# The first MoE block in full fp32 on whole decoded weights, norm sums in banks of their own, weight loads as steps of their own, and a new order

## The chip, the core and the metric

One NeuronCore of a Trainium2 chip. Its engines work side by side, each through its own queue in order: TensorE (PE; its weight loads are shown apart, as PEld), VectorE (DVE), ScalarE (ACT), GpSimd (POOL), and SyncE (SP), which issues most of the DMAs. The metric is the device time of one execution in microseconds (us).

## What is computed

Attention with a delta rule over 768 steps for 4 x 8 heads of 48 features, and two MoE blocks on the 3072 tokens that come out of it:

```python
k_n = k / (np.linalg.norm(k, axis=-1, keepdims=True) + 1e-06)
for t in range(S):                       # S = 768, state 48 x 48 per head
    y[:, :, t] = einsum('bhd,bhde->bhe', q[:, :, t], state)
    v_old = einsum('bhde,bhd->bhe', state, k_n[:, :, t])
    state = state + beta_t * einsum('bhd,bhe->bhde', k_n[:, :, t], v_t - v_old)
# first MoE block: d_model 384, d_ff 2048
h = x @ w_in
g = where(h >= 1, h, where(h <= -1, 0, (h + 1) ** 2 / 4))
x = g @ w_out
# second: d_ff 1536
xn = x / sqrt(mean(x * x) + 1e-06) * rms_g
out = (silu(xn @ w_gate) * (xn @ w_val)) @ w_out
```

The MoE weights arrive as 64-bit floats and are decoded to fp32 on the chip.

## The kernel before

**Attention.** The 768 steps are cut into 12 chunks of 64. A unit `u` is one chunk of one half of the heads (p = u % 2, chunk c = u // 2). Groups of units (`GRP`: 0-1, 2-3, then four at a time) share their coefficients. `a_ss` forms the squared norms of k, `a_coef` the root, reciprocal and coefficients, `a_gram` the products k k^T (`gk`), `inverse` (POOL, groups from 2 on) or `inv16` and `inv_t` (groups 0 and 1) the inverse of a triangular matrix, `a_mz` and `a_mw` its second half (`mg`). The state goes on from chunk to chunk: `b_gs` (`gs`), `b_tr` (`tr`), `b_x` (`px`, the chunk's output), `b_ds` (the state), and `b_xT` turns the output over (`xps`) into the tokens `xh`, `xl` of the MoE.

**First MoE block** (`m1`). Tokens go in blocks `BLK`: block 0 is chunk 0 (256 tokens), block 1 is chunk 1, then two chunks (512 tokens) at a time. For each of 16 slices f of d_ff: a first half, `mm_in`, 3 contraction steps into `hps`; ACT and DVE form `g`; a second half, `mm_out`, 3 products into `acc`. Every fp32 product is made of three fp32r products (`mm3`): high x high, high x low, low x high. So weights, tokens and `g` are split into a high and a low part. Block 0's products are 256 columns wide.

**Weights.** `w_dec` loads one weight tile (SP), forms it with three copies on ACT and one instruction on DVE (`dy`), then its high part (ACT or DVE) and low part (DVE or POOL). There are 32 tiles for the first block (`w[1, f, i]`, i = 0 for the first half, 1 for the second) and 36 for the second, which go back to DRAM.

**Second block** (`m2`). Products of 512 columns (`gv`, `acc`), paced by PE.

**Order.** A planner (`Flow`) writes the order of all this. Each step names its engine, a cost, what it needs and which buffers it takes and frees; a step's priority is its place in the program plus a number of the table `PLACE`; `CHAIN` names the first steps of a kind that go ahead of all. The order is then fixed: each engine works through its queue and waits where an operand isn't there. Where the planner sees a gap on PE ahead of the MoE, `spin` puts filler products (`warm`) there. `early` makes a tile of the pool `wp` (32 buffers), which later holds the weights.

## Time and profile before

| | before |
|---|---|
| timed runs (3), median and ends | 1093.87 us (1091.93 to 1099.88) |
| the profiled execution | 1093.34 us |
| its span in the trace | 1091.6 us |
| mean granted TensorE clock | 0.987 |
| busy: PE, DVE, ACT, POOL | 1070.5, 614.2, 526.0, 301.4 us |
| HBM read, written | 83.33, 32.77 MB |

Busy time of PE counts filler products, and the ends of its matmuls are modelled: a busy PE isn't PE at its peak. What a stage is bound by is read from the windows and the timelines of that stage, from the start of one instruction to the start of the next. In the trace a full fp32 product makes two records (x32 are 16 products), an fp32r product one.

### The profile page before, as it was taken

The numbers are of one execution on the slowest core, as the hardware profiler recorded it, in microseconds if no ns is written. First come the engines' busy times: TensorE is split into PE (matmuls) and PEld (weight loads), VectorE is DVE, ScalarE is ACT, GpSimd is POOL, SyncE is SP. The second block draws the span as 40 slices with busy tenths as digits, with TensorE's granted clock in tenths as the row PEclk, the third lists the DMA queues.
The fourth block names the chain that finished last, engine by engine and source line by source line (L and its number), as shares of the span: only waits on it lengthen the run. The fifth ranks groups of instructions, "written<-read, shape, count | busy, mean of one in ns | idle before, by whom it ended". The sixth has DMA issues, their size and how long they took to land.

```text
span 1091.6 us, 23723 instructions
## 1 busy us (share of the span) xinstructions
PE 1070.5 (98%) x9804; PEld 894.6 (82%) x9804; DVE 614.2 (56%) x1068; ACT 526.0 (48%) x999; POOL 301.4 (28%) x500
## 2 busy tenths in 40 slices
PE   8888999999999999999999999999999999999998
PEld 6678899878888878888888888888888888888887
DVE  5788998676687666755555533633333333333332
ACT  4787876556567656555666532522222122222221
POOL 5769587286683862011000000000000000000000
PEclk8998899999999999999999999999999999999999
DMA  9794456855648445334224930110010010010000
GB/s 285 261 290 129 76 163 224 215 161 141 159 144 167 143 121 171 95 106 122 102 73 166 343 109 10 39 39 20 1 39 20 1 49 11 20 39 0 29 1 30
DMA packets 140876, 117.64 MB, mean 108 GB/s; under 512 B 97120, under 2 KB 106976, under 8 KB 140768
## 3 DMA queue, kind: packets, MB, share of 16 engines
q1 hardware_dynamic: 120208, 113.50, 34.4%
q10 hardware_dynamic: 20560, 2.62, 1.6%
q8 instruction: 77, 1.26, 0.5%
q14 instruction: 31, 0.25, 0.1%
HBM read 83.33 MB, written 32.77 MB: 106 GB/s over the span
## 4 chain that ended last, share of the span: by engine, by line
PE 87%; DVE 4%; POOL 4%; ACT 2%; issue 2%; DMA 0%; SPq 0%; POOLq 0%; DVEq 0%; ACTq 0%
PE acc L884 10%; PE acc L885 10%; PE acc L886 10%; PE gv L886 9%; PE gv L885 9%; PE gv L884 9%; PE hps L884 6%; PE hps L885 5%; PE hps L886 5%; PE gs L748 3%; PE tr L824 2%; POOL xi L659 2%; POOL tmp L653 2%; PE gk L512 2%; PE px L837 2%
## 5 line engine op out<-in xcount | busy, mean ns | idle before, releaser
L884 PE MATMUL acc<-g,w 128*128 128x512 f32 (+1 forms) x552 | 209.4, 379 | 2.8 <-ACT da L356 2.8
L886 PE MATMUL acc<-g,w 128*128 128x512 f32 (+1 forms) x552 | 205.4, 372 | 0.3 <-DVE w L372 0.2
L885 PE MATMUL acc<-g,w 128*128 128x512 f32 (+1 forms) x552 | 205.5, 372 | 0.0
L884 PE MATMUL gv<-fix,w 128*128 128x512 f32 x432 | 168.2, 389 | 0.0
L886 PE MATMUL gv<-fix,w 128*128 128x512 f32 x432 | 168.2, 389 | 0.0
L885 PE MATMUL gv<-fix,w 128*128 128x512 f32 x432 | 168.2, 389 | 0.0
L901 ACT ACTIVATE g<-fix 128x512 fp32r<-128x512 f32 x72 | 45.4, 631 | 213.3 <-PE acc L886 207.4
L884 PE MATMUL hps<-xh,w 128*128 128x512 f32 (+1 forms) x336 | 127.1, 378 | 1.8 <-DVE s L924 1.8
L902 DVE TENSOR_TENSOR g<-fix,g 128x512 fp32r<-128x512 f32 x72 | 49.9, 693 | 133.1 <-ACT g L901 133.1
L884 PEld LDWEIGHTS acc<-g,w 128*128 128x128 f32 x552 | 104.3, 189 | 22.2 <-ACT da L356 3.0
L885 PE MATMUL hps<-xl,w 128*128 128x512 f32 (+1 forms) x336 | 122.3, 364 | 0.0
L886 PE MATMUL hps<-xh,w 128*128 128x512 f32 (+1 forms) x336 | 122.2, 364 | 0.0
L886 PEld LDWEIGHTS acc<-g,w 128*128 128x128 f32 x552 | 104.3, 189 | 18.8 <-DVE w L372 0.7
L885 PEld LDWEIGHTS acc<-g,w 128*128 128x128 f32 x552 | 104.4, 189 | 16.8
L921 ACT ACTIVATE s<-hps 128x512 f32<-128x512 f32 (+1 forms) x112 | 59.7, 533 | 104.4 <-PE hps L886 86.7
L924 DVE TENSOR_TENSOR s<-s,hps 128x512 f32<-128x512 f32 (+1 forms) x112 | 67.9, 607 | 68.2 <-ACT s L922 67.0
L1132 DVE TENSOR_TENSOR fix<-fix,gv 128x512 f32<-128x512 f32 x72 | 49.5, 688 | 87.4 <-ACT fix L1131 87.4
L653 POOL TENSOR_TENSOR tmp<-nt,xi 128x31 f32<-128x31 f32 (+15 forms) x155 | 92.9, 599 | 20.3 <-DMA nt<-scr_a 8.7
L659 POOL TENSOR_TENSOR xi<-xi,tmp 128x31 f32<-128x31 f32 (+15 forms) x155 | 93.9, 606 | 12.1
L932 DVE TENSOR_TENSOR g<-s,g 128x512 fp32r<-128x512 f32 (+1 forms) x111 | 78.8, 716 | 29.6 <-ACT g L930 28.8
L885 PEld LDWEIGHTS gv<-fix,w 128*128 128x128 f32 x432 | 81.1, 188 | 16.9
L884 PEld LDWEIGHTS gv<-fix,w 128*128 128x128 f32 x432 | 81.1, 188 | 16.8
(186 smaller groups left out, 1673.3 us busy)
## 6 DMA issues: line engine op xcount, KB each, us to landing
wst<-in_w SPq DMA_DIRECT2D x68, 384.0 KB, 5.4
w2d<-wst SPq DMA_DIRECT2D x36, 384.0 KB, 4.6
w<-w2d SPq DMA_DIRECT2D x36, 384.0 KB, 3.7
kvb<-in_kv SPq DMA_DIRECT2D x24, 384.0 KB, 3.7
kt<-in_kqT SPq DMA_DIRECT2D x22, 256.0 KB, 4.7
scr_a<-al SPq DMA_DIRECT2D x20, 256.0 KB, 5.9
xn_d<-x SPq DMA_DIRECT2D x12, 384.0 KB
xn<-xn_d SPq DMA_DIRECT2D x18, 256.0 KB, 3.7
```

What stands on the lines that cost most here:

```text
L653: nc.gpsimd.tensor_tensor(out=tv, in0=nt[:, m:32, j:m].to_broadcast([w, n, m]), in1=x[:, j:m, 0:m].to_broadcast([w, n, m]), op=ALU.mult,)
L659: nc.gpsimd.tensor_tensor(out=x[:, m:32, 0:m], in0=x[:, m:32, 0:m], in1=tv, op=ALU.add)
L748: nc.tensor.matmul(out=ps[half(b), h, 0:n], lhsT=kt[u][half(1 - b), 4 * k + h, :], rhs=qs[p][half(1 - b), b, 4 * k + h, 0:n], start=True, ...
L884: nc.tensor.matmul(out=out, lhsT=wh, rhs=xh, start=first, stop=False, skip_group_check=shared)
L885: nc.tensor.matmul(out=out, lhsT=wh, rhs=xl, start=False, stop=False, skip_group_check=shared)
L886: nc.tensor.matmul(out=out, lhsT=wl, rhs=xh, start=False, stop=last, skip_group_check=shared)
L901: nc.scalar.activation(out=hi, in_=src, func=ACTF.Copy)
L902: nc.vector.tensor_tensor(out=lo, in0=src, in1=hi.bitcast(F32), op=ALU.subtract)
L921: nc.scalar.activation(out=s, in_=ps, func=IDENTITY_SAT240, scale=240.0)
L924: nc.vector.tensor_tensor(out=s, in0=s, in1=ps, op=ALU.max)
L932: nc.vector.tensor_tensor(out=g[:, 1, :], in0=s, in1=g[:, 0, :].bitcast(F32), op=ALU.subtract)
L1132: nc.vector.tensor_tensor(out=sg, in0=sg, in1=ps[0], op=ALU.mult)
```

## The change

Block 0 (j = 0) uses whole fp32 weights (`w1y`, [128, 2, 384] for both halves of f), whole tokens and whole `g`: one full fp32 product where three fp32r products stood. `w_dec` of the first block now ends with the whole weight; the parts for the later blocks are formed by a step of its own, `w_fin`, whose last instruction comes behind block 0's use of the weight. The load is a step of its own too, `w_ld`. The first of the three copies of the decode may go to ACT, POOL or DVE. The norm sums of units 0 to 7 (4 before) are formed on PE, as products 32 or 8 columns wide (1 before); group 0's have a bank of their own. Three layouts on DVE are turned (`a_gram`, `inv_t`). Costs of some steps and the whole table of places are other ones. Cut to its core (`PLACE` has new numbers all through; a line stands for it):

```diff
-    CHAIN = {"a_coef": 8, "a_gram": 1, "a_mw": 7, "a_mz": 9, "a_ss": 11, "b_ds": 4, "b_gs": 4, "b_load": 23, "b_q": 6, "b_tr": 4, "b_vn": 4, "b_x": 28, "b_xT": 18, "inv16": 5, "inv_t": 8, "inverse": 1, "ka_load": 13, "m1_rms": 16, "w_in": 24, "x_load": 3}
-    DRAIN, SWITCH, KEEP, STAY, AHEAD = 0.15, 0.16, 270.76, 24.18, 0.29
+    CHAIN = {"a_gram": 4, "a_mw": 1, "a_mz": 14, "a_ss": 7, "b_ds": 12, "b_gs": 11, "b_load": 13, "b_q": 7, "b_tr": 12, "b_vn": 8, "b_x": 31, "b_xT": 15, "inv_t": 8, "inverse": 2, "ka_load": 24, "m1_rms": 9, "w_fin": 2, "w_ld": 6, "x_load": 17}
+    DRAIN, SWITCH, KEEP, STAY, AHEAD = 0.15, 0.16, 167.04, 28.86, 0.2
...
-        "a_coef": (157.4, 48.4, -4, -28.1, 27.2, -36.1, -5.8),
+        "a_coef": (1.1, 6.8, -17.1, 18.6, -17.4, -17.2, 54.5),
...
-    one = cst([128, 1], "one")
+    one = cst([128, 32], "one")
...
+    def w_dec(n, f, i):
+        yield S("ACT", 0.55, [("w_ld", n, f, i)], ("dec",), alt=[("POOL", 1.0), ("DVE", 0.5)] if n == 1 else [], sb=True)
...
+        if fl.eng == "ACT":
+            nc.scalar.activation(out=y.bitcast(F32), in_=w_hi, func=ACTF.Copy, scale=2.0**-112)
+        else:
+            (nc.gpsimd if fl.eng == "POOL" else nc.vector).tensor_scalar(out=y.bitcast(F32), in0=w_hi, scalar1=2.0**-112, scalar2=None, op0=ALU.mult)
+        yield S("ACT", 1.06)
...
+            o = w1y[f][:, i, :].bitcast(U32)
...
+        nc.vector.scalar_tensor_tensor(out=o, in0=y, scalar=3, in1=a, op0=ALU.logical_shift_left, op1=ALU.bitwise_or)
+        dac.append(a)
+        if n == 1:
+            return
...
+    def w_fin(f):
+        home = "wp" if f < NF1 - 1 else "stg"
+        for i in range(2):
+            yield S("ACT", 0.52, [("w_dec", 1, f, i)], ("wp",), alt=[("DVE", 0.4)], sb=True)
+            y = w1y[f][:, i, :]
+            t = w1t[f, i] = wp.tile([128, 2, DM], F32R, name="w", tag="w")
+            hi, lo = t[:, 0, :], t[:, 1, :]
...
+            yield S("DVE", 0.57, [("m1", 0, f, 0), ("m1", 0, f, 3)] if i else (), (), (home,) if i else (), alt=[("POOL", 1.0)], sb=True)
+            (nc.gpsimd if fl.eng == "POOL" else nc.vector).tensor_tensor(out=lo, in0=y, in1=hi.bitcast(F32), op=ALU.subtract)
...
-    EARLY, NORM = 8, 4
+    EARLY, NORM = 8, 8
...
+                if g == 0:
+                    nm = ap_.tile([128, 2 * H, 32], F32, name="nm", tag="at")
+                else:
+                    nm = norms[:, 0:128] if g == 1 else norms[:, 128:384]
...
-                    nc.tensor.matmul(out=ss_t[g][half(b), i, h:h + 1], lhsT=kk[half(1 - b), h, :], rhs=one[half(1 - b)], start=True, stop=True)
+                    nc.tensor.matmul(
+                        out=nrm[g][half(b), H * i + h, :], lhsT=kk[half(1 - b), h, :], rhs=one[half(1 - b), 0:8 if g else 32], start=True, stop=True
+                    )
...
-                out=e1.rearrange("p s m -> p m s"), in0=ps.rearrange("p h (x s) -> p (h x) s", s=16),
...
+                out=e1, in0=ps.rearrange("p h (x s) -> p s (h x)", s=16),
...
-                    out=o2.rearrange("p t (x s) -> p t x s", x=2), in_=inv["x", c].unsqueeze(2).to_broadcast([128, 16, 2, 16])
+                    out=o2.rearrange("p (x s) t -> p t x s", x=2), in_=inv["x", c].unsqueeze(2).to_broadcast([128, 16, 2, 16])
...
+        if c == 0:
+            nc.scalar.activation(out=hi.bitcast(F32), in_=ps, func=ACTF.Copy)
+            return
...
+            if whole:
+                nc.tensor.matmul(out=ps, lhsT=w[:, ks], rhs=xh[:, k, 0:n].bitcast(F32), start=k == 0, stop=k == KD - 1)
...
+        if j == 0:
+            yield S("DVE", 0.42, (), ("g",), ("h", "s"))
+            g = g_tile(w)
+            nc.vector.tensor_tensor(out=g[:, 0, :].bitcast(F32), in0=s, in1=ps, op=ALU.max)
...
-        spin(2.6)
-        fl.free["PE"] = 6.9
+        spin(1.0)
+        fl.free["PE"] = 5.1
```

What the new order is shows in three places. The first is the start of PE's queue: `norms` and `nm` are the norm sums, `gk` the grams, `gs` the first products of chunk 0. Before:

```order
L1019 MATMUL warm<-ident 128x512 x2
L1019 MATMUL warm<-ident 128x256
L443 MATMUL norms<-one,kk 64x1 x16
L512 MATMUL gk<-kt 64x64 x16
L443 MATMUL norms<-one,kk 64x1 x48
L512 MATMUL gk<-ka 64x64 x16
```

Now:

```order
L1087 MATMUL warm<-ident 128x384
L557 MATMUL gk<-kt 64x64 x16
L487 MATMUL nm<-one,kk 64x32 x16
L557 MATMUL gk<-kt 64x64 x16
L487 MATMUL nm<-one,kk 64x32 x16
L487 MATMUL norms<-one,kk 64x8 x16
L1087 MATMUL warm<-ident 128x256
L793 MATMUL gs<-qs,kt 64x64 x32
```

The sums of units 0 and 1 and their grams now lead, and the sums of units 2 and 3 have moved behind them.

The second is DVE's chain to the inverse of group 0 (`inv_o<-gk` is a scaled gram). Before:

```order
L475 TENSOR_TENSOR mcoef_92<-nn,mdiag 128x64
L516 TENSOR_TENSOR inv_o<-gk,mcoef_92 128x32x16
L523 TENSOR_TENSOR inv_e<-inv_o 128x16x16
L462 TENSOR_SCALAR n__324<-n__324 128x16
L464 RECIPROCAL r<-n__324 128x16
L454 TENSOR_REDUCE ss<-kk 128x8
L516 TENSOR_TENSOR inv_o<-gk,mcoef_92 128x32x16
```

Now:

```order
L520 TENSOR_TENSOR mcoef_92<-nn,mdiag 128x64
L561 TENSOR_TENSOR inv_o<-gk,mcoef_92 128x512
L568 TENSOR_TENSOR inv_e<-inv_o 128x16x16
L561 TENSOR_TENSOR inv_o<-gk,mcoef_92 128x512
L568 TENSOR_TENSOR inv_e<-inv_o 128x16x16
L606 STREAM_TRANSPOSE inv_o<-inv_e 128x512
```

Group 1's coefficients and a norm sum that stood between the two scaled grams have moved behind the inverse.

The third is PE around the 16th first half of block 0 (`wst` is the whole weight of f = 15, `wy` of the others; `w` is a weight in two parts, for block 1). Now:

```order
L943 MATMUL hps<-xh,wy 128x256 x3
L951 MATMUL acc_1238<-g,wy 128x256
L951 MATMUL acc_1239<-g,wy 128x256
L951 MATMUL acc_1240<-g,wy 128x256
L943 MATMUL hps<-xh,wst 128x256 x3
L557 MATMUL gk<-ka 64x64 x16
L933 MATMUL hps<-xh,w 128x256
L934 MATMUL hps<-xl,w 128x256
L935 MATMUL hps<-xh,w 128x256
```

Each half of block 0 is three products where nine stood; block 1 begins right behind its last first half, on weights in parts.

## Rows read from the trace of the kernel before

**Rows 1.** The page: span and instructions.

```profile
span 1091.6 us, 23723 instructions
```

**Rows 2.** Windows: by stage busy us (instructions) of each engine, granted clock, DMA.

```profile
core 0: us, PE busy (x) PEld busy (x) DVE busy (x) ACT busy (x) POOL busy (x), PEclk, DMA share, GB/s
0.00:63.00 63.00, 55.86 (x1018) 41.19 (x1019) 44.75 (x96) 38.95 (x84) 38.67 (x88) 0.92 0.84 267
63.00:136.00 73.00, 64.44 (x960) 59.91 (x959) 64.06 (x118) 61.43 (x137) 54.23 (x82) 0.91 0.59 158
136.00:206.00 70.00, 70.00 (x1305) 66.55 (x1303) 56.57 (x119) 47.88 (x112) 46.74 (x83) 1.00 0.65 188
206.00:1091.00 885.00, 880.21 (x6527) 726.96 (x6526) 448.84 (x738) 377.73 (x666) 161.74 (x248) 1.00 0.29 86
```

**Rows 3.** Timeline of PE, 0 to 64: start us, us, records, [idle <-releaser].

```profile
3.38 4.63 PE L1019 MATMUL warm<-ident 128*128 128x512 f32 x6 [3.38 <-POOL ident masks.py:199]
7.95 1.24 PE L443 MATMUL norms<-one,kk 64*64 64x1 f32 x32
9.05 1.13 PE L512 MATMUL gk<-kt 64*64 64x64 f32 x32
...
30.57 1.14 PE L778 MATMUL tr<-kvb,dt 64*64 64x48 f32 x32 [1.77 <-DVE dt L626]
31.63 6.47 PE L1019 MATMUL warm<-ident 128*128 128x512 f32 x12
38.04 1.14 PE L778 MATMUL tr<-kvb,dt 64*64 64x48 f32 x32
...
63.02 0.58 PE L884 MATMUL hps<-xh,w 128*128 128x256 f32 x1
63.43 0.28 PE L885 MATMUL hps<-xl,w 128*128 128x256 f32 x1
63.55 0.28 PE L886 MATMUL hps<-xh,w 128*128 128x256 f32 x1
```

**Rows 4.** Timeline of DVE, 12 to 32 us.

```profile
12.37 0.17 DVE L462 TENSOR_SCALAR n__276<-n__276 128x16 f32<-128x16 f32 x1 [2.51 <-ACT n__276 L460]
...
16.12 0.17 DVE L462 TENSOR_SCALAR n__324<-n__324 128x16 f32<-128x16 f32 x1
...
17.82 1.05 DVE L516 TENSOR_TENSOR inv_o<-gk,mcoef 128x512 f32<-128x512 f32 x1 [0.83 <-PE gk L512]
...
29.05 2.26 DVE L626 TENSOR_TENSOR dt<-inv_o,mcoef 128x256 f32<-128x256 f32 x4
```

**Rows 5.** Timeline of PEld: weight loads of 512-column filler products.

```profile
40.58 0.19 PEld L1019 LDWEIGHTS warm<-ident 128*128 128x128 f32 x1 [0.24 <-issue]
41.01 0.19 PEld L1019 LDWEIGHTS warm<-ident 128*128 128x128 f32 x1 [0.24 <-issue]
```

**Rows 6.** Lines by form, ACT, 63 to 136: busy, mean ns | idle.

```profile
L354 ACT ACTIVATE dy<-wst 128x384 f32<-128x384 f32 x21 | 11.5, 550 | 0.9 <-DVE w L372 0.9
L930 ACT ACTIVATE g<-s 128x256 fp32r<-128x256 f32 x15 | 5.9, 408 | 1.0 <-DVE s L924 0.7 <-PE acc L886 0.3
```

**Rows 7.** Lines by form, DVE, 63 to 136 us.

```profile
L372 DVE TENSOR_TENSOR w<-dy,w 128x384 fp32r<-128x384 f32 x21 | 15.7, 746 | 0.5
L370 DVE CAST w<-dy 128x384 fp32r<-128x384 f32 x23 | 11.7, 510 | 0.5
L932 DVE TENSOR_TENSOR g<-s,g 128x256 fp32r<-128x256 f32 x13 | 8.8, 691 | 0.6 <-ACT g L930 0.6
L924 DVE TENSOR_TENSOR s<-s,hps 128x256 f32<-128x256 f32 x15 | 6.1, 412 | 1.2 <-ACT s L922 1.1
```

**Rows 8.** Timeline of PE, 134 to 137 us.

```profile
135.53 0.28 PE L886 MATMUL hps<-xh,w 128*128 128x256 f32 x1
```

**Rows 9.** Timeline of POOL: group 2 inverse begins; its result is used.

```profile
73.32 0.25 POOL L653 TENSOR_TENSOR tmp<-nt,xi 128x31 f32<-128x31 f32 x1
...
129.35 0.68 POOL L680 TENSOR_TENSOR wt<-tx,c 128x256 f32<-128x256 f32 x1 [4.16 <-DMA tx<-scr_x]
```

More of the change, by code (lines that the diff above doesn't have):

```diff
@@ L397, in kernel_body @@
     tx_t = {}
-    ss_t = {}
+    ss_t, nrm = {}, {}
     wt = {}
@@ L500, in a_gram @@
         bank = "at" if g > 1 else f"ea{u % 3}"
-        yield S("PE", 0.97, [("ka_load", x) for x in ((u, u ^ 1) if ew and g else (u,) if ew else (u // 2 * 2,))] + ([("a_gram", u - 1, 0)] if u % 2 and not ew else []), (bank,), () if u < 4 else ("wp",) if ew else ("ka",) if u % 2 else ())
+        yield S("PE", 0.97, [("ka_load", x) for x in ((u, u ^ 1) if ew and g else (u,) if ew else (u // 2 * 2,))] + ([("a_gram", u - 1, 0)] if u % 2 and not ew else []) + ([("a_ss", u, 0)] if 4 <= u < NORM else []) + ([("a_coef", g)] if g > 1 else []), (bank,), () if u < 4 else ("wp",) if ew else ("ka",) if u % 2 else ())
         t = ka_t[u]
```

176 lines of the change are left out of this document (102 added, 74 removed), and 33 rows, old and new, of the table PLACE.

## Prediction

> **What bounds the kernel now.** The profiled execution took 1093.34 us, of which the trace spans 1091.6 [rows 1]; the three timed runs have their median at 1093.87, half a microsecond off, so the sum below is made against 1093.3. The windows by stage come first. From 136 us on PE is busy in 950.2 of 955 us, at full clock in the windows [rows 2]: whatever stands behind that point is paced by TensorE. Before it things differ. Until 63 us there is no product of the MoE at all: PE's 55.9 busy us are small attention products and filler (the `warm` products), while chunk 0 goes through a chain of engines. Between 63 and 136 us the products of block 0 run, but ACT is busy 61.4 and DVE 64.1 of 73 us [rows 2], decoding weights, and PE waits in its queue for a weight here and a `g` there; its granted clock averages 0.91 in this stage and in the one before, so part of it ran at 1.2 instead of 2.4 GHz. The bound is therefore two stages long: the chain of chunk 0, then the decode on ACT and DVE; after that TensorE.
>
> From this comes the method. Take one point on PE: the end of the 16th first-half product group of block 0 (f = 15), which before ends at 135.53 + 0.12 = 135.65 us [rows 3, 8]. Ahead of it PE's queue holds nearly the same work in both kernels: the same 16 first halves, 13 second halves and all of chunks 0 and 1 (64 `gs` products of chunk 1, 32 `px`, 32 `ds`), with one more attention group or so either way. What follows it is almost the same work too. So the end moves by as much as this point moves, plus what the work behind it grows.
>
> **The change, part by part.**
>
> *Whole products.* Three products of 256 columns become one in full fp32. The old ones start 0.12 us apart [rows 3], so three take 0.36. A full fp32 product of 512 columns shows in the trace as two records, whose loads start 0.43 apart [rows 5]; 256 columns should take the same two records at half the length, 2 x 0.215 = 0.43. It isn't shown with 256 columns and new weights each time. Bounds: 0.36 below (the three it replaces; I see no reason for less), and 0.43 + 2 x 0.19 = 0.81 above, if neither of its two weight loads (0.19 each [rows 5]) hides behind a product. I take 0.43, since the filler's loads lie inside the product's time. 96 of them in block 0 cost 96 x 0.07 = 6.7 us more of PE; 87 stand ahead of the point (6.1 us) and 9 behind it (0.6). The Trainium skill, "FP8 and Floating Point Precision", section "TensorE Precision Notes", says true fp32 needs four passes through the array. By four passes of 0.12 us the growth would be 96 x 0.12 = 11.5 us, not 6.7, an estimate from that page; the filler's rows agree on four passes, but at 0.107 us each, so the sum keeps 6.7.
>
> *Norm sums.* Group 0's sums now have a bank of their own, 32 columns wide, and units 2 to 7 share another, 8 wide. Before, the root of group 0 was taken at 12.2 us, after 96 records of sums and 32 of grams [rows 3, 4]; now 64 and 64, and unit 2 no longer stands ahead of it. PE starts at 3.4 us; 384 filler columns at the pace of the first row (1280 in 4.6 us) take 1.4, two groups of grams and two of sums about 1.1 each [rows 3], 4.4 together, and up to twice that at 1.2 GHz. So 9.2 to 13.6; I take 10, a gain of 2 us (between -1.5 and 3). The other 128 sum products (64 more in all, about 1.1 us per 32 records, so 4.4 us at most) stand where filler stood: no cost, and up to 4.4 us if they don't.
>
> *DVE's chain.* Between the first and second scaled gram of group 0 DVE did group 1's coefficients and a sum and waited for a gram, 16.1 to 17.8 us [rows 4]. All that is behind the inverse now: 1.7 us. The rewritten layouts of the scaled gram, of the transpose and of `dt` aren't shown; four instructions of 1.05, 1.05, about 0.7 and 1.1 us, I leave as they are; half or double gives -2 to +4 us. Then `dt` comes at 30.5 - 2 - 1.7 = 26.8.
>
> *Filler.* Before, the second unit's `tr` waited behind 6.4 us of filler (31.63 to 38.04), though its `dt` was there at 31.3 [rows 3, 4]. Now both `tr` stand together, and all filler ahead of block 0 shrinks from 10240 to 5888 columns. The second `tr` ends near 28.5 instead of 39: 10.5 us. From there on to the first product it was 24 us before; the chain of copies and small products is the same, with 2944 filler columns for 3456 (about -1 us) and without the low part of x (-1.3 us, but the last filler of 768 columns stands there). ACT can hold this back: 77 instructions stand up to chunk 0's second copy, 82 before, and ACT has less idle time to hide them. I take 52.5 us for the first product instead of 63.0, between 50 and 58.
>
> *Decode.* Of the 19 weights that ACT works on between the first and the 16th `s`, it does the first of three copies for 8 (DVE for 9, POOL for the rest); the split of `g` is gone, and high and low part come later (`w_fin`). By the order between those two points: ACT loses 13 copies of 0.55, 4 more of 0.6 and 15 `g` of 0.41, and gains 6 parts, 4 squares and one root of about 0.5 [rows 6]: 61.4 - 15.7 + 5.5 = about 51. DVE loses 15 `s` of 0.41, 16 x 0.28 as `g` gets the cheaper form (0.69 to 0.41), 5 casts of 0.51 and 4 subtractions of 0.75, and gains 9 copies priced as casts (0.51), 4 instructions of about 0.7 (three `al`, one decode step), 4 `dt` and a transpose (3.0 [rows 4]), and 8 small ones of 0.4 [rows 7]: 64.1 - 16.2 + 13.6 = about 62. So ACT falls by ten, DVE hardly at all, and PE's own work in the stretch goes up by 6.1. If DVE kept its share of before (64.1 of 73), the stretch would take 70.5; what should raise it is that a weight no longer goes ACT, DVE, ACT, DVE, and that its parts are filling work. Below, DVE's own 62. I take 68.
>
> *Sum.* 52.5 + 68 = 120.5 for the point, 15.1 earlier than 135.65. Behind it stand 0.6 us more of whole products; the order of the rest of PE has as many changes between small and full products (178 for 175), and the number of decoded second-block weights at each f of the first is the same within two or three, so I give it nothing. 1093.3 - 15.1 + 0.6 = **1078.8**.
>
> A limit from the other side: the first `mg` of chunk 2 waits for POOL's inverse of group 2, which began at 73.3 and let POOL go on at 129.4 us [rows 9]. It starts behind the masks of chunk 1, before 10.3 us after the first product [rows 3, 9], now some 14 with whole products between, so near 67; it takes some 3 us longer with what was put into it, and its result comes near 126. PE's `mg` stands about 10 us behind the point, at 131: it just fits, and an earlier point than 116 gains nothing.
>
> **Rivals.**
> *Half of it.* ACT is the bound from the start: first product at 57, and DVE's share stays, stretch of 71. For it: DVE's work is nearly that of before, ACT's count ahead of the first product too. Point at 128, end 1093.3 - 7.7 + 0.6 = 1086.
> *Given back.* The point moves, but block 1 then waits for its two parts: 11 to 13 low parts are still to be formed on DVE and POOL at 0.75 to 1.2 us beside block 1, with DVE busy 57 of 70 us there already [rows 2, 7]; 13 x 1.26 (cast and subtraction) = 16 us, of which 13 fit. With an inverse that is 5 us late: 1078.8 + 3 + 5 = 1087.
> *All of it.* First product at 50, stretch of 64: limited by `mg` to 116, 1093.3 - 19.7 + 0.6 = 1074.
> *Slower.* The weight loads of whole products don't hide: 0.81 us each, 96 x 0.38 = 36 us more, of which the 6 us that PE waits for DVE take some: 1078.8 + 30 = 1109. It decides from 0.59 us a product on (96 x 0.16 = 15). Against it: the filler's loads lie inside its products [rows 5], though that is the same weight each time. The Trainium skill, "TensorE: Matmul & The Clock Gate", section "Weight-path perf modes", says that the fast weight load is not used for FP32. That speaks for this rival; in these rows the fp32 load takes 0.19 us, and no row shows it exposed.
>
> **Chances.** Forecast 0.54 (1074.5 to 1083), half of it 0.23, given back 0.10, all of it 0.08, slower 0.05. A measurement of this kernel can tell about 1% (10.9 us): faster means under 1082.4, slower over 1104.3. Faster: 0.52 of the forecast and 0.08; slower: 0.05; the rest is within. The range leaves out the slower case and the tails of the halves: 1070 to 1090.
>
> **What would show it.** Right: a root of group 0 near 10 us and `dt` near 27; first whole product between 50 and 55, whole products 0.43 apart (two records of 0.215); f = 15 of block 0 done near 120; DVE the busiest engine until then; PE without gaps behind it. Wrong: whole products over 0.5 us; ACT without idle time from 12 us to the first product; PE waiting for a `w` of `w_fin` or for `mg`'s operands between 120 and 190; any gap on PE after 206 that wasn't there.

## The result, and the profile of the changed kernel

The changed kernel takes 1084.03 us (median of four runs, 1081.6 to 1085.78) against 1094.82 before (four runs): ratio 0.9895, 95% interval 0.9852 to 0.9938. A second set, beside the experiments, gave 1086.81 (four runs, 1084.35 to 1089.58) against 1095.23: 0.9915 (0.9883 to 0.9947). So the change makes the kernel about 1% faster, 8 to 11 us. It was forecast to, with 1078.8 as the figure; the measured medians are 5 and 8 us above that. They lie inside the forecast's range (1070 to 1090), but above the band of its own case (1074.5 to 1083), and above the 1082.4 under which the prediction would call the kernel faster. That it is faster, by less than that, the two intervals show.

The span of the profiled execution fell from 1091.6 [rows 1] to 1081.6 us. The windows by stage, cut as in [rows 2] (busy us and instructions of each engine, granted clock, DMA):

```profile
core 0: us, PE busy (x) PEld busy (x) DVE busy (x) ACT busy (x) POOL busy (x), PEclk, DMA share, GB/s
0.00:63.00 63.00, 55.47 (x1148) 45.02 (x1150) 44.63 (x99) 42.76 (x94) 39.90 (x78) 0.95 0.83 267
63.00:136.00 73.00, 67.92 (x916) 57.56 (x917) 62.16 (x122) 53.26 (x116) 58.20 (x103) 1.00 0.57 154
136.00:206.00 70.00, 69.48 (x1287) 65.37 (x1286) 55.73 (x114) 45.06 (x101) 47.65 (x80) 1.00 0.75 207
206.00:1081.00 875.00, 871.81 (x6472) 718.28 (x6470) 437.19 (x719) 376.12 (x664) 160.83 (x247) 1.00 0.29 85
```

Against [rows 2]: from 63 to 136 us ACT has 8 us less to do, VectorE 2 less, PE and POOL 3.5 and 4 more, and the clock is at full speed. Behind 136 us little has changed: PE is busy for over 99% of both windows, and the last one is 10 us shorter. Now PE's timeline (start us, us, records, [idle <-releaser]), for the places of [rows 3, 8]:

```profile
28.35 3.65 PE L823 MATMUL tr<-kvb,dt 64*64 64x48 f32 x64 [0.62 <-DVE dt L671]
31.77 1.55 PE L831 MATMUL tr<-dt,off 64*64 64x64 f32 x32
...
44.21 0.87 PE L848 MATMUL tr<-z,y 32*32 32x48 f32 x32
47.17 0.92 PE L896 MATMUL ds<-z,kvb 64*48 64x48 f32 x32 [2.10 <-ACT dy L364]
...
55.68 2.54 PE L943 MATMUL hps<-xh,wy 128*128 128x256 f32 x11
...
123.86 1.56 PE L943 MATMUL hps<-xh,wst 128*128 128x256 f32 x6 [0.18 <-DVE g L982]
125.36 0.86 PE L557 MATMUL gk<-ka 64*64 64x64 f32 x22
```

Both `tr` stand together now. The first whole product is at 55.68 (63.02 before), and the 16th first half ends where the next row begins, at 125.36 (135.65 before). This end is "the point" of the prediction, and it is called so below. The point moved by 10.3 us and the span by 10.0.

VectorE's timeline, for the rows that answer to [rows 4]:

```profile
12.21 0.69 DVE L561 TENSOR_TENSOR inv_o<-gk,mcoef 128x512 f32<-128x512 f32 x1
12.93 1.25 DVE L568 TENSOR_TENSOR inv_e<-inv_o 128x256 f32<-128x256 f32 x1
14.29 0.69 DVE L561 TENSOR_TENSOR inv_o<-gk,mcoef 128x512 f32<-128x512 f32 x1
15.01 0.43 DVE L568 TENSOR_TENSOR inv_e<-inv_o 128x256 f32<-128x256 f32 x1
...
26.25 1.04 DVE L663 STREAM_TRANSPOSE inv_o<-x 128x512 f32<-128x512 f32 x1
27.33 1.43 DVE L671 TENSOR_TENSOR dt<-inv_o,mcoef 128x256 f32<-128x256 f32 x4
```

The wait between the two scaled grams is gone, and `dt` comes at 27.33 for 29.05.

The experiments found that the row to read first is one on which the prediction says nothing. It stands in ACT's timeline. POOL's row shows what ACT waits for, and POOL's two other rows show where its two long inverses of the head begin:

```profile
110.59 0.52 ACT L495 ACTIVATE kk<-kk 128x384 f32<-128x384 f32 x1 [2.94 <-DVE qs L812]
117.47 2.04 ACT L706 ACTIVATE nt<-xi 128x1024 f32<-128x1024 f32 x1 [6.36 <-POOL xi L704]
119.40 0.38 ACT L977 ACTIVATE s<-hps 128x256 f32<-128x256 f32 x1
```

```profile
51.81 0.22 POOL L616 TENSOR_TENSOR inv_e<-nt,x 128x15 f32<-128x15 f32 x1 [3.55 <-DVE nt L607]
...
72.94 0.44 POOL L698 TENSOR_TENSOR tmp<-nt,xi 128x31 f32<-128x31 f32 x1
...
117.19 0.25 POOL L704 TENSOR_TENSOR xi<-xi,tmp 128x31 f32<-128x31 f32 x1
```

From 111.1 to 117.47 ACT does nothing. The next instruction in its queue is the copy of POOL's inverse of group 2, which ends at 117.44. Behind that copy stand the squares (`s`) of the 13th to 16th first half; the row at 119.40 is the 13th's. PE's 15th first half waits for the 13th's `g`, which VectorE forms from them:

```profile
120.83 1.56 PE L943 MATMUL hps<-xh,wy 128*128 128x256 f32 x6 [1.39 <-DVE g L982]
```

In the kernel before, the same copy began at 117.39, but ACT came to it without any idle time.

### The profile page after: what moved, and what is told of

It reads as the page before. It is cut to its first block, busy times and chain, and to the rows that moved or that the text cites. A ratio compares the mean times of both kernels' runs of the same rounds, so it can differ in the third digit from the quotient of the medians.

```text
span 1081.6 us, 23711 instructions
## 1 busy us (share of the span) xinstructions
PE 1064.7 (98%) x9818; PEld 886.2 (82%) x9818; DVE 599.7 (55%) x1050; ACT 517.2 (48%) x973; POOL 306.6 (28%) x506
## 4 chain that ended last, share of the span: by engine, by line
PE 89%; POOL 6%; DVE 2%; issue 1%; DMA 0%; ACT 0%; SPq 0%; POOLq 0%; DVEq 0%; ACTq 0%
PE acc L933 11%; PE acc L934 10%; PE acc L935 10%; PE gv L934 9%; PE gv L933 9%; PE gv L935 9%; PE hps L933 6%; PE hps L934 5%; PE hps L935 5%; PE gs L793 3%; PE px L882 2%; PE tr L869 2%; POOL xi L704 2%; POOL tmp L698 2%; PE ds L896 1%
## 5 line engine op out<-in xcount | busy, mean ns | idle before, releaser
L933 PE MATMUL acc<-g,w 128*128 128x512 f32 (+1 forms) x504 | 194.9, 387 | 0.0
L934 PE MATMUL acc<-g,w 128*128 128x512 f32 (+1 forms) x504 | 191.3, 380 | 0.0
L935 PE MATMUL acc<-g,w 128*128 128x512 f32 (+1 forms) x504 | 191.2, 379 | 0.0
L933 PE MATMUL hps<-xh,w 128*128 128x512 f32 (+1 forms) x288 | 111.7, 388 | 1.1 <-DVE g L982 1.1
L933 PEld LDWEIGHTS acc<-g,w 128*128 128x128 f32 x504 | 94.7, 188 | 18.9
L935 PEld LDWEIGHTS acc<-g,w 128*128 128x128 f32 x504 | 94.7, 188 | 18.2
L934 PEld LDWEIGHTS acc<-g,w 128*128 128x128 f32 x504 | 94.8, 188 | 16.7
L934 PE MATMUL hps<-xl,w 128*128 128x512 f32 (+1 forms) x288 | 107.3, 373 | 0.0
L935 PE MATMUL hps<-xh,w 128*128 128x512 f32 (+1 forms) x288 | 107.1, 372 | 0.0
L993 DVE TENSOR_TENSOR s<-s,hps 128x512 f32<-128x512 f32 (+1 forms) x96 | 61.4, 640 | 74.3 <-ACT s L978 73.7
L1203 DVE TENSOR_TENSOR fix<-fix,gv 128x512 f32<-128x512 f32 x72 | 49.5, 687 | 87.3 <-ACT fix L1202 87.3
L698 POOL TENSOR_TENSOR tmp<-nt,xi 128x31 f32<-128x31 f32 (+15 forms) x155 | 89.0, 574 | 26.3 <-DMA nt<-scr_a 15.9
L933 PEld LDWEIGHTS gv<-fix,w 128*128 128x128 f32 x432 | 81.1, 188 | 17.0
L935 PEld LDWEIGHTS gv<-fix,w 128*128 128x128 f32 x432 | 81.1, 188 | 16.8
L934 PEld LDWEIGHTS gv<-fix,w 128*128 128x128 f32 x432 | 81.1, 188 | 16.7
```

Source lines behind the costliest of these rows:

```text
L698: nc.gpsimd.tensor_tensor(out=tv, in0=nt[:, m:32, j:m].to_broadcast([w, n, m]), in1=x[:, j:m, 0:m].to_broadcast([w, n, m]), op=ALU.mult,)
L933: nc.tensor.matmul(out=out, lhsT=wh, rhs=xh, start=first, stop=False, skip_group_check=shared)
L934: nc.tensor.matmul(out=out, lhsT=wh, rhs=xl, start=False, stop=False, skip_group_check=shared)
L935: nc.tensor.matmul(out=out, lhsT=wl, rhs=xh, start=False, stop=last, skip_group_check=shared)
L993: nc.vector.tensor_tensor(out=s, in0=s, in1=ps, op=ALU.max)
L1203: nc.vector.tensor_tensor(out=sg, in0=sg, in1=ps[0], op=ALU.mult)
```

## The experiments

All twelve runs are one execution with a profile each; `again`, `poolA` and `ntpool` were timed in more. The table has the readings that decide, in us, from the traces: T1 is the start of the first whole product (of the first product in the kernel before), "inverse" the end of POOL's inverse of group 2.

| run | T1 | inverse | point | point - T1 | point - inverse | span | end - point |
|---|---|---|---|---|---|---|---|
| before | 63.02 | 117.11 | 135.65 | 72.6 | 18.5 | 1091.6 | 955.9 |
| after | 55.68 | 117.44 | 125.36 | 69.7 | 7.9 | 1081.6 | 956.2 |
| again (after, unedited) | 61.01 | 122.27 | 130.16 | 69.2 | 7.9 | 1086.3 | 956.1 |
| pe10 | 58.72 | 118.86 | 133.57 | 74.9 | 14.7 | 1089.2 | 955.6 |
| dve10 | 57.20 | 120.27 | 128.87 | 71.7 | 8.6 | 1084.7 | 955.8 |
| act10 | 60.54 | 123.58 | 132.19 | 71.7 | 8.6 | 1093.2 | 961.0 |
| thin | 56.93 | 116.80 | 124.75 | 67.8 | 8.0 | 1082.5 | 957.8 |
| short | 58.60 | 112.69 | 123.74 | 65.1 | 11.1 | 1080.5 | 956.7 |
| poolA | 57.41 | 115.64 | 125.59 | 68.2 | 10.0 | 1081.8 | 956.2 |
| tr6 | 59.99 | 123.23 | 131.14 | 71.2 | 7.9 | 1094.9 | 963.7 |
| ntpool | 59.78 | 120.09 | 131.32 | 71.5 | 11.2 | 1088.0 | 956.7 |
| lay | 59.55 | 120.70 | 129.83 | 70.3 | 9.1 | 1086.6 | 956.8 |
| one1 | 60.06 | 123.03 | 130.93 | 70.9 | 7.9 | 1091.0 | 960.1 |
| bcut (of before) | 63.77 | 117.36 | 135.99 | 72.2 | 18.6 | 1091.8 | 955.8 |

### Which engine paces the stretch from T1 to the point

The first theory was that PE's own work does. Three runs add some 10 us to one engine, one takes 12.5 us from PE. `pe10`:

```diff
-        mm_in(ps, w1t[f, 0] if j else w1y[f][:, 0, :], xt[j], j == 0)
+        for _ in range(2 if j == 0 and f % 2 else 1):
+            mm_in(ps, w1t[f, 0] if j else w1y[f][:, 0, :], xt[j], j == 0)
```

> The changed kernel with the first-half product group of every odd f of block 0 issued twice: 8 groups of 3 whole products, 8 x 1.30 = 10.4 us more of TensorE between the first whole product (55.68 us) and the end of the 16th first half (125.36 us). The result stays the same. Theory: in the changed kernel TensorE's own work paces this stretch (its queue shows only three gaps over 0.7 us in it), so each added microsecond comes out: the 16th first half ends 8 to 10.4 us later, at 133 to 136, and the run ends as much later, about 1090 to 1092 as span. Rival: the decode on ScalarE and VectorE still paces the stretch, as I took it in the prediction; then the added products fill gaps, and the end moves by less than 5 us.

`dve10` and `act10` put these two lines ahead of VectorE's last step of the decode (shift and or) and of ACT's copy of the low half-words:

```diff
+        wst[n] = wst.get(n, 0) + 1
+        for _ in range(2 if n == 1 and 12 <= wst[n] <= 27 else 1):
```

> The changed kernel with the last step of the decode (shift and or, VectorE) done twice for the 12th to 27th of the 32 weights: 16 x 0.62 = about 10 us more of VectorE in the same stretch. The result stays the same. Theory (TensorE paces the stretch): VectorE is idle 12 of its 69.7 us, so less than 4 us come out at the end of the 16th first half (at most 129.5), and no more at the end of the run. Rival (the decode paces it): 7 to 10 us come out (132.5 to 135.5).

> The changed kernel with one of ScalarE's two decode copies (the low half-words) done twice for the 12th to 27th weight: 16 x 0.615 = about 10 us more of ScalarE in the same stretch. The result stays the same. Theory (TensorE paces the stretch): ScalarE is idle 14.5 of 69.7 us; less than 4 us come out at the end of the 16th first half (at most 129.5). Rival (the decode paces it): 7 to 10 us come out.

`thin`, in the loops over the three products of a half:

```diff
             if whole:
+                if k == 1:
+                    continue
...
             if whole:
+                if e == 1 and not first and not last:
+                    continue
```

> The changed kernel with the middle one of three products left out in every first half of block 0, and in every second half but the first and the last: a third of the sums of block 0 is missing. 16 + 13 products of 0.43 us, 12.5 us, are gone ahead of the end of the 16th first half. Theory (TensorE paces the stretch): that end comes 8 to 12 us earlier, at 113 to 117. The run's end follows it only by 1 to 4 us, since the first mg product of chunk 2 waited for its operands already (0.5 us at 137.7): its operands come over VectorE's sums, POOL's inverse (which ended at 117.4) and two transfers, and none of these gets faster, so PE should now wait some 8 us at the mg. Rival 1 (the decode paces the stretch): the 16th first half moves by less than 4 us. Rival 2 (the operands of mg come earlier with the rest): the end of the run moves as the 16th first half, by 8 to 12 us.

Measured by the length of the stretch (T1 itself differs between executions, below): 10.4 us more on PE lengthen it by 5.2 (74.9 for 69.7), the steps added on VectorE or on ACT by 2.0 each (busy time of these engines in it rose by 11.3 and 8.1 us), and 12.5 us less on PE shorten it by 1.9 only. Neither theory holds as it stands. PE's own work is not all that paces it, or `thin` would have shown it. The decode on ACT and VectorE isn't either, or the steps added would have cost most of their time. Where ACT stands in `thin` points to a third. Its timeline, and the end of PE's stretch:

```profile
116.83 1.97 ACT L706 ACTIVATE nt<-xi 128x1024 f32<-128x1024 f32 x1 [9.05 <-POOL xi L704]
```

```profile
123.69 1.13 PE L945 MATMUL hps<-xh,wst 128*128 128x256 f32 x4 [1.57 <-DVE g L986]
124.75 1.15 PE L557 MATMUL gk<-ka 64*64 64x64 f32 x32
```

ACT stands 9.05 us at the copy, and the point comes 7.95 us after the end of the inverse. In the changed kernel it was 7.92. That is a new theory: POOL's inverse of group 2, through ACT's queue, sets the point. `pe10` shows the other bound: there the inverse was over 14.7 us before the point, ACT stood only 0.9 us at the copy, and PE waited nowhere in the stretch (busy 74.85 of 74.85 us). Without the 8 x 1.30 us of double products it is 74.85 - 10.4 = 64.4 us. That is what PE itself needs.

`dve10` and `act10` have 8.6 us from the inverse to the point, both, but that alone is no sign of this tie. In `dve10` 0.8 of the 5.6 us that PE waits stand behind the copy. In `act10` PE waits nowhere behind it. From 71 us on its clock was low for 3.4 us, and its 4.5 us of waiting stand earlier than the copy and are for ACT itself, to whose work the edit added. The two longest (total us, times, longest):

```profile
PE gs L795 <- ACT qs L805: 2.4, 1, 2.4
PE tr L850 <- ACT y L842: 1.4, 1, 1.4
```

The other half of `thin`'s expectation, that the end would not follow the point because of chunk 2's `mg`, could not be tested: the point hardly moved.

### The new theory, the control, and the filler

`short` takes 8 of 31 steps out of POOL's inverse of group 2:

```diff
             yield S("POOL", 1.2 * (0.36 + n * m * 0.004))
+            if g == 2 and j in range(8, 24, 2):
+                continue
```

> The changed kernel with 8 of the 31 steps of POOL's inverse of group 2 left out (the inverse of chunks 2 and 3 is then not the right one): 11 to 13 us less of POOL. In the changed kernel ACT stands 6.4 us at its copy of that inverse (117.47), with the squares of the 14th to 16th first half queued behind it; and the end of the 16th first half came 7.9, 8.0, 8.6 and 8.6 us after the end of that inverse in the changed kernel and in three of the four edited ones. Theory: POOL's inverse, through ACT's queue, sets this point, and TensorE's own work is close behind (the stretch with 10.4 us of double products took 74.8 us, so 64.4 without). Then the inverse ends at 104 to 107, ACT doesn't wait for it, and the 16th first half ends 64 to 66 us after the first whole product, 120 to 122.5; the mg of chunk 2 comes earlier too, and the run ends 3.5 to 5.5 us earlier than the unedited one. Rival: the decode holds this point anyway, and the wait of ACT only stands in place of another; the point moves by less than 1.5 us and the end too.

The inverse ended 54.1 us after T1 (61.8 before the edit), ACT stood 0.9 us for 6.36, and the stretch came to 65.1 us, in the forecast 64 to 66. Its rows on ACT and PE:

```profile
112.72 2.03 ACT L708 ACTIVATE nt<-xi 128x1024 f32<-128x1024 f32 x1 [0.90 <-POOL xi L706]
```

```profile
58.60 1.67 PE L945 MATMUL hps<-xh,wy 128*128 128x256 f32 x7
...
122.36 1.46 PE L945 MATMUL hps<-xh,wst 128*128 128x256 f32 x6
123.74 1.15 PE L557 MATMUL gk<-ka 64*64 64x64 f32 x32
```

So taking time from POOL brings the stretch to what `pe10` says PE needs; PE waits 0.5 us in it, for 4.3 in the first trace. But the copy is only a part of that. Of the 4.3 us, 1.6 stand behind the copy, and 2.2 at `tr` of chunk 1. There VectorE had waited for another inverse of POOL, that of chunk 1, which `short` leaves alone. PE's row and VectorE's in the first trace:

```profile
73.92 2.07 PE L823 MATMUL tr<-kvb,dt 64*64 64x48 f32 x64 [2.25 <-POOL xi L704]
```

```profile
71.10 1.06 DVE L663 STREAM_TRANSPOSE inv_o<-x 128x512 f32<-128x512 f32 x1 [2.39 <-POOL x L622]
```

In the control (next) PE waits 3.7 us, 2.5 of them behind the copy and none at this `tr`. So by PE's waits the theory holds for the end of the stretch, and the copy is worth 1.6 to 2.5 us. That the rest of the 4.0 to 4.5 us by which the stretch of `short` is shorter belongs to the edit isn't shown. Nor does the run tell ACT's queue from what VectorE may lose beside a busy POOL.

The end didn't come 3.5 to 5.5 us earlier than in the first trace, but 1.0, since T1 came 2.9 later. The control says whether that belongs to the edit.

> The changed kernel once more, unedited, as the measure for the edits. In the four edited runs the first whole product came between 56.9 and 60.5 us, with the granted clock at 0.5 for 6.8 us or more between 45 and 58 us, which the first trace of the changed kernel does not have there. If that belongs to the edits, the trace of this run looks like the first one (first whole product within 0.5 us of 55.7, end of the 16th first half within 1 us of 125.4). If it is a matter of the single execution, it may differ by 1 to 3 us in the first and by less in the second, and the span with it.

It does not. The same program had T1 at 61.01, 5.3 us later than in its first trace, and a span 4.8 longer; point - T1 (69.2), point - inverse (7.9) and end - point (956.1) are the same within 0.5. PE's rows and the windows:

```profile
49.54 1.52 PE L896 MATMUL ds<-z,kvb 64*48 64x48 f32 x32 [2.64 <-issue]
...
61.01 1.24 PE L943 MATMUL hps<-xh,wy 128*128 128x256 f32 x5
```

```profile
46.00:57.00 11.00, 8.36 (x165) 6.58 (x163) 6.28 (x12) 5.33 (x12) 4.86 (x9) 0.69 0.60 180
```

Two things make the difference (the granted clock has two levels here, 1.00 for 2.4 and 0.50 for 1.2 GHz). The root of the norms came 1.4 us later (12.06 for 10.67) and `dt` 2.6 (29.94 for 27.33). Then the granted clock was at the lower level for 6.8 us from 49.5 on, right behind PE's idle time ahead of `ds`; PE worked there without a gap to the first product, and its 32 `ds` took 1.45 us for 0.86. With 6.8 us at half the clock the path from `tr` to the first product took 3.6 us longer. The first trace has an idle time there too (2.10 us ahead of 47.17, above) and no fall behind it. Nine of the twelve traces of the changed kernel and its edits have one that begins between 45 and 50 us; the first trace is without, and so are `tr6` and `one1`, whose clock was low earlier and longer.

`tr6` puts filler back where the kernel before had it:

```diff
+            if u == 1:
+                spin(5.2)
             ps = [ap_.tile([128, H, C], F32, name="tr", tag="at")]
```

> The changed kernel with 12 filler products (2560 columns, about 5.2 us) put back between the first tr of unit 0 and that of unit 1, where the kernel before had 6.4 us of filler. The result stays the same. My account of the prediction gave 10.5 us of the gain to this filler and to both tr standing together. Theory: the first whole product comes 4.5 to 5.5 us later and the 16th first half 4 to 5.5 us later, since POOL's inverse of chunk 1 starts behind a step of VectorE that stands behind that chain; the run ends 4 to 5.5 us later. Rival: POOL's and the decode's work go on beside the filler, the inverse of group 2 ends within 1.5 us of 117.4, and the end moves by less than 2 us.

T1 came at 59.99, which is 4.3 later than in the first trace and 1.0 earlier than in the control. Counted from `dt` it is 33.1 us, in the traces with an unedited head 28.4 to 33.1. The run doesn't separate the theories. It took longest of all for another reason, far behind the point; PE's row, and the window around it:

```profile
168.64 0.37 PE L557 MATMUL gk<-ka 64*64 64x64 f32 x2 [2.95 <-issue]
```

```profile
165.00:182.00 17.00, 14.05 (x201) 13.11 (x198) 8.45 (x21) 3.89 (x11) 15.43 (x24) 0.70 0.53 168
```

PE stood 2.95 us there with nothing the profile shows to wait for, then ran at the lower level for 10.2 us; end - point is 963.7 for 956.

`bcut` is the same question asked of the kernel before, whose filler ahead of the second `tr` it cuts from 6.4 us to 1:

```diff
             n = max(0, int((gap - 0.2) / 0.23))
+            n = 4 if n == 21 else n
```

> The kernel before, with 17 of 21 units of the filler between its two first tr left out (6.4 us of it become about 1). Theory of the prediction: the chain to the first product and the decode stand one behind the other, so the second tr comes 5 us earlier, the first product at 58 instead of 63.0, the end of the 16th first half 4 to 5 us earlier than 135.65, and the run ends as much earlier, near 1088. Rival: in the kernel before the decode on ACT and VectorE starts before this chain ends and paces the stretch behind it by itself; then the first product comes 4 to 5 us earlier, but the 16th first half by less than 2 and the run too.

The first product came at 63.77, not at 58, and the point at 135.99. Neither theory had that. PE's rows, and the window behind the second `tr`:

```profile
29.94 1.13 PE L778 MATMUL tr<-kvb,dt 64*64 64x48 f32 x32
31.00 1.13 PE L1020 MATMUL warm<-ident 128*128 128x512 f32 x2
34.71 1.95 PE L778 MATMUL tr<-kvb,dt 64*64 64x48 f32 x32 [2.58 <-DVE al L537]
```

```profile
34.00:41.00 7.00, 6.29 (x68) 4.72 (x69) 6.86 (x13) 6.06 (x14) 6.17 (x10) 0.51 0.97 326
```

The second `tr` came 3.3 us earlier than the 38.04 of [rows 3], not 5: PE waited 2.6 us for VectorE's `al`, which stands behind other work in VectorE's queue. In this wait the clock fell (from 34.0 us, for 6.8; in the kernel before from 32.2, for 3.4), and PE's next products took up to twice as long. So the filler was cover for a wait on VectorE; taken out alone it brought nothing in this execution. That the longer fall comes from the missing filler isn't shown: falls differ as much between two executions of one program (above).

### Two tries at a faster version

`poolA` gives VectorE the causal masks of chunk 1 and four scalings of `kvb`:

```diff
-                nc.scalar.activation(out=qs[p][half(b), b, h4, 0:C], in_=ps[half(b), :, 0:C], func=ACTF.Copy)
+                if c:
+                    m = mask[half(b)].unsqueeze(1).to_broadcast([64, 4, C])
+                    nc.vector.tensor_tensor(out=qs[p][half(b), b, h4, 0:C], in0=ps[half(b), :, 0:C], in1=m, op=ALU.mult)
+                else:
+                    nc.scalar.activation(out=qs[p][half(b), b, h4, 0:C], in_=ps[half(b), :, 0:C], func=ACTF.Copy)
             yield S("POOL", 1.1)
-            for b in range(2):
+            for b in range(0 if c else 2):
...
-        nc.gpsimd.tensor_tensor(out=v, in0=v, in1=bc(coef[g][0][:, i, :], D), op=ALU.mult)
+        (nc.vector if 2 <= u < 6 else nc.gpsimd).tensor_tensor(out=v, in0=v, in1=bc(coef[g][0][:, i, :], D), op=ALU.mult)
```

> The changed kernel with work of chunk 1 taken from POOL and given to VectorE: the causal masks (8 selects of 0.41 on POOL and 8 copies of about 0.39 on ACT become 8 products with the mask on VectorE, 0.43 each as for the later chunks) and four scalings of kvb (0.83 to 1.14 on POOL). 6.9 us less of POOL, 3 us less of ACT, about 5.5 us more of VectorE. The result stays the same. Theory (POOL's inverse of group 2 sets the end of the 16th first half): the inverse ends 4 to 7 us earlier, at 110.5 to 113.5, the 16th first half at 120 to 122, and the run ends 3 to 5 us earlier than the unedited one, about 1079 by the times. Rival: POOL gains nothing, since VectorE's queue is late with these and POOL's short steps slow down beside it; the inverse ends within 2 us of 117.4 or later, and the run is equal or slower.

The inverse ended 58.2 us after T1, 3 us earlier than in the unedited traces, for 6.9 us less of work: POOL now waited 4.9 us for a transfer (`nt<-scr_a`) at the start of the inverse. The stretch fell by 1.0 to 1.5, to 68.2. The point stood 10 us behind the inverse, so that no longer bound it. PE's and ACT's waits in the stretch (total us, times, longest):

```profile
PE gs L793 <- DVE qs L805: 1.9, 2, 1.6
```

```profile
ACT nt L706 <- POOL xi L704: 1.4, 1, 1.4
```

ACT's wait shrank from 6.4 to 1.4, and PE got a new one of 1.9 us for VectorE's masks early in the stretch. It took 1083.26 us (four runs, ratio to before 0.9891, 0.9868 to 0.9914), the unedited kernel in the same set 1086.81 (0.9915, 0.9883 to 0.9947). The intervals overlap: that it beats the changed kernel isn't shown.

`ntpool` takes the copy out of ACT's queue:

```diff
+        if g == 2:
+            nc.gpsimd.tensor_copy(nt, x.rearrange("p t s -> p s t"))
+        else:
             nc.scalar.activation(out=nt, in_=x.rearrange("p t s -> p s t"), func=ACTF.Copy)
...
-        nc.scalar.dma_start(out=scr_x[g].rearrange("s x u h t -> (x u h) s t"), in_=nt)
+        (nc.sync if g == 2 else nc.scalar).dma_start(out=scr_x[g].rearrange("s x u h t -> (x u h) s t"), in_=nt)
...
-            (nc.gpsimd if fl.eng == "POOL" else nc.vector).tensor_scalar(out=y.bitcast(F32), in0=w_hi, scalar1=2.0**-112, scalar2=None, op0=ALU.mult)
+            (nc.gpsimd if fl.eng == "POOL" and f < NF1 - 1 else nc.vector).tensor_scalar(out=y.bitcast(F32), in0=w_hi, scalar1=2.0**-112, scalar2=None, op0=ALU.mult)
```

> The changed kernel with one copy moved: the copy of the finished inverse of group 2, 2.04 us on ACT at 117.47 with the squares of three first halves queued behind it, is done by POOL itself, and its transfer issued by SP; POOL's last decode step (1.2 us, for the last weight) goes to VectorE, so that it doesn't stand behind the copy. The result stays the same. Theory: it is this place in ACT's queue that ties the end of the 16th first half to the end of POOL's inverse (7.9 us apart in the unedited kernel, twice). Without it the stretch from the first whole product to that end takes 65 to 66.5 us, as in the run with the shortened inverse (65.15), instead of 69.2 to 69.7; the run ends 2.5 to 4.5 us earlier than the unedited kernel (1084.0 and 1086.8 in two sets), at about 1081 to 1083. What can take a part: four low parts of block 1 stand behind the copy on POOL and come some 2 us later. Rival: the inverse holds the end through the mg of chunk 2 as well (in the unedited kernel it waited 0.5 us); then the point comes earlier and the mg waits by as much, and the run takes as long as the unedited kernel.

No gain: 1087.39 us (six runs, 1083.53 to 1089.72; 0.9914, 0.9891 to 0.9937). ACT no longer waits for the inverse, but in the trace (of the slowest of the six) the tie came back through VectorE. POOL's row, VectorE's rows and PE's:

```profile
120.99 1.94 POOL L707 COPY nt<-xi 128x1024 f32<-128x1024 f32 x1
```

```profile
119.58 0.40 DVE L411 CAST w<-wy 128x384 fp32r<-128x384 f32 x1
121.08 2.07 DVE L411 CAST w<-wy 128x384 fp32r<-128x384 f32 x1 [1.11 <-POOL w L413]
...
123.93 0.41 DVE L985 TENSOR_TENSOR g<-s,hps 128x256 f32<-128x256 f32 x1
```

```profile
124.40 2.93 PE L946 MATMUL hps<-xh,wy 128*128 128x256 f32 x6 [3.12 <-DVE g L985]
127.12 2.77 PE L954 MATMUL acc<-g,wy 128*128 128x256 f32 x6
```

A cast that takes 0.40 us ahead of the copy and 0.35 behind it took 2.07 beside it, and ended 0.2 us after it. The Trainium skill, "SBUF — State Buffer", section "Who interferes with whom", says that VectorE in its two-port modes, which a cast can enter, contends with GpSimd for a port pair that they share: whoever issues first holds it for the whole instruction, and the other blocks. These two rows agree with it; which mode the cast was in, the trace doesn't show. The cast and what follows it stood ahead of `g` of the 13th first half, for which PE's 15th waited 3.1 us. In this wait the clock fell to the lower level, for 6.8 us, and PE's next two groups took 2.7 and 2.6 us for 1.3 (from one start to the next). Without the wait and the fall the stretch would be near 66 (an estimate, 71.5 - 3.1 - 2.6), where it was expected; no run shows that. Neither of the expected cases: not the `mg`, but the engine beside POOL.

### Layouts and norm sums

`lay` turns VectorE's new layouts in the head back; `one1` makes the norm sums one column wide again:

```diff
-                out=e1, in0=ps.rearrange("p h (x s) -> p s (h x)", s=16),
+                out=e1.rearrange("p s m -> p m s"), in0=ps.rearrange("p h (x s) -> p (h x) s", s=16),
...
-            o2 = part(inv["o", c], 0, [128, 32, 16])
+            o2 = part(inv["o", c], 0, [128, 16, 32])
```

> The changed kernel with the layouts of VectorE's head turned back to those of the kernel before: the scaled gram, the second transpose and the dt of the inverse. The result stays the same. In the two traces the scaled gram takes 0.69 us and 1.05 before, and the four dt instructions of chunk 0 1.43 and 2.26. My prediction left this term at nothing (-2 to +4). Theory: it is a real gain of 0.36 x 2 + 0.83 and what the transposes differ, about 1.5 to 2 us; from the root of the norms to the end of chunk 0's second dt it takes 17.4 us in the unedited kernel (10.67 to 28.09; 18.6 in its second trace), and here 19 to 20.5, and the first whole product comes as much later. Rival: VectorE's steps of the inverse beside POOL are what counts, and the layouts' share is under 0.7 us.

VectorE's timeline, the same steps as shown of the changed kernel:

```profile
11.92 1.05 DVE L561 TENSOR_TENSOR inv_o<-gk,mcoef 128x512 f32<-128x512 f32 x1
13.00 1.11 DVE L568 TENSOR_TENSOR inv_e<-inv_o 128x256 f32<-128x256 f32 x1
...
26.15 0.71 DVE L663 STREAM_TRANSPOSE inv_o<-x 128x512 f32<-128x512 f32 x1
26.89 2.06 DVE L671 TENSOR_TENSOR dt<-inv_o,mcoef 128x256 f32<-128x256 f32 x4
```

Line by line the new layouts save 0.36 on each scaled gram and 0.63 on the four `dt`, and lose 0.33 on the transpose: 1.0 us. From the root to the end of the four `dt` it takes 18.6 us here (10.38 to 28.96) and 17.9 to 19.3 in the traces with the layouts as changed. A gain of 1 us drowns in what VectorE's steps beside POOL vary by (the first `L568` takes 1.25 us in the changed kernel, the second 0.43). The rival (under 0.7) is nearer.

```diff
-                        out=nrm[g][half(b), H * i + h, :], lhsT=kk[half(1 - b), h, :], rhs=one[half(1 - b), 0:8 if g else 32], start=True, stop=True
+                        out=nrm[g][half(b), H * i + h, 0:1], lhsT=kk[half(1 - b), h, :], rhs=one[half(1 - b), 0:1], start=True, stop=True
```

> The changed kernel with its norm sums one column wide again (before: one; changed: 32 for group 0, 8 for units 2 to 7), banks and order unedited. The result stays the same. The sums cost 28 to 52 ns a record at 32 columns, 30 at 8, and 28 to 36 in the kernel before, so TensorE's time for them stays the same within 1 us. What the width may do is to the clock: before, the granted clock fell to 0.5 at 11.7 us for 6.8 us, in the middle of the sums and grams; in none of the six traces of the changed kernel and its edits does it fall ahead of 23 us. Theory: the width keeps it up; with one column the clock falls ahead of 20 us, and the root of the norms or dt comes 1 to 3 us later. Rival: the width has no part in it; the clock's first fall is at 23 to 29 us again, and the root comes at 10 to 12 us as in the others.

Two windows of this run, ahead of the first fall of the clock and over it:

```profile
0.00:26.00 26.00, 22.62 (x388) 18.86 (x390) 13.38 (x35) 13.03 (x29) 16.73 (x37) 1.00 0.95 311
26.00:41.00 15.00, 15.00 (x181) 11.20 (x180) 10.84 (x22) 5.75 (x13) 5.48 (x12) 0.54 0.57 196
```

The clock stayed at full speed until 26.7, so the width isn't what keeps it up in the first 20 us; there the rival holds. It then stayed low for 13.7 us, longer than in any other trace (0 to 10.2), and the sums and filler queued ahead of `tr` ran until 33.77, 2.8 us after the last `dt`. One execution can't say whether that belongs to the width. The run's end has a fall at 170 us as `tr6` has, and can't be used.

## Why the prediction was right, and where its sum was off

**The method held.** The point set the end: end - point is 955.6 to 956.8 in ten of the fourteen traces and 957.8 in an eleventh; in the other three PE stood for 2 to 3 us near 169 us and then ran at the lower clock (last section). Between before and after it grew by 0.2 us, where 0.6 was forecast. Behind 136 us PE waits once in the changed kernel, 0.5 us at the `mg`; "given back" is out.

**Whole products.** 0.43 us as taken: three of them take 1.30 (116.69 to 117.98 in PE's queue), new weights each time, their loads hidden. "Slower" is out. The 6.1 us ahead of the point cost little by themselves: `thin` took twice that away and got 1.9. The Trainium skill, "FP8 and Floating Point Precision", section "TensorE Precision Notes", counts four passes for true fp32. The trace shows two records and 0.43 us a product, 3.6 times the 0.12 us of an fp32r product, so it fits four passes of 0.107 each, and the 11.5 us that 0.12 a pass would have given were too many.

**The sum failed in T1.** Forecast 52.5; measured 55.68 and 61.01. The forecast has both `tr` over at 28.5, and 24 us from there. They were over at 31.8 and 33.5, and 23.9 and 27.5 us followed. So the step that failed in both traces is the path up to "The second `tr` ends near 28.5":

- The root (forecast 10) came at 10.67 and 12.06.
- The 1.7 us to be saved in "DVE's chain" didn't come out. From the root to `dt` it took 16.7 and 17.9 us, and 16.9 in the kernel before (12.15 to 29.05), although the wait between the scaled grams is gone and their layouts, which I left "as they are", saved 0.7. The first six steps of VectorE's inverse took it back: 3.4 us from 17.14 on in the first trace, 1.4 before (from 21.41). POOL is busy beside them; that this is the cause isn't shown. That `dt` came at 27.33 where 26.8 stands is luck: the 26.8 is counted from 30.5, where [rows 3] have the first `tr`, and the row of `dt` is at 29.05 [rows 4]. It gained 1.7 us in the first trace, not 3.7, and lost 0.9 in the control.
- The two `tr` (64 records) took 3.42 us in the first trace, at the lower clock, and 1.87 in `thin` (28.34 to 30.21), at full speed. I took the durations as they stood and didn't ask which of them ran at which clock, though [rows 2] show a mean of 0.92 in that stage.

Behind `tr`, "the chain of copies and small products is the same" held in the first trace; in the control the lower clock from `ds` on made it longer. `bcut` adds that the 6.4 us of filler weren't a cost that could be taken out alone.

**The stretch** was forecast at 68 and is 69.7 and 69.2 (72.6 before). The size was near, the reason wrong. It was argued from VectorE's share; what sets it is PE's own work, 64.4 us, and on top of it waits, most of them for POOL: its inverse of chunk 1 at `tr`, and its inverse of group 2, which ends 61.3 to 61.8 us after T1 and lets ACT go on. I had the inverse in "a limit from the other side", with a start near 67, a result near 126 and the `mg` as the place where it counts. It started at 72.94, as late as before [rows 9], because the inverse of chunk 1 ahead of it began at 51.81 (40.26 before): it waits 3.55 us for a step that VectorE does behind its sums for `ds`. The place where it counts is ACT's queue, 12 us ahead of the `mg` (which waited 0.5 us at 137.67). The rival "half of it" (point at 128, 1086) came close in time, with the points at 125.4 and 130.2 and the second median at 1086.81, but not by its cause: ACT was idle 14.5 of 69.7 us, and with 8.1 us more of it the stretch grew by 2.0. The clock stood in no term of the stretch either: before, its mean was 0.91 in that stage [rows 2], by which some 13 of the 73 us ran at the lower level (an estimate from that mean); in the first trace of the changed kernel it is 1.00.

With measured terms the sum closes. First trace: 1078.8 + 3.2 (T1) + 1.7 (stretch) - 0.4 (behind) = 1083.3, and that execution took 1083.27. Control: 1078.8 + 8.5 + 1.2 - 0.4 = 1088.1, and it took 1088.03. Since T1 and the stretch add up to the point, this tests only that nothing changes behind it. The medians, 1084 and 1087, lie between these two executions, as they would with a T1 between theirs; the others have no trace.

**What stays open.** How much of the gain each part brings. No run takes the new order back by itself. That the lighter decode shortens the stretch from 72.6 is consistent with 61.4 us of ACT's work from 63 to 136 us before [rows 2] and 53.3 now, but no run took it alone; neither did one show what paced the stretch of the kernel before. Why the clock falls behind some 2 us of idle time in one execution of a program and not in another is open as well.

## What to carry to other kernels

When an engine becomes lighter, look in every queue for an instruction that waits for a slow engine and stands ahead of work for the fast one: here one copy on ACT tied PE to POOL, visible as 6.4 us of ACT's idle time, while POOL's busy share said nothing. Then price it by what the pacing engine waits behind it: 1.6 to 2.5 us on PE, not 6.4. A constant distance between two events (8.6 us in `act10`) is no tie as long as nothing waits. Before a chain's durations are carried over from one kernel to the next, mark which of them ran at the lower clock; filler that looks like a cost can be cover for a wait. And profile the same program twice before reading a few microseconds out of one trace.
